# One attention order for two head pairs: read-outs in two groups, maxima through SyncE, more masks on TensorE

## The chip, the cores and the metric

One NeuronCore of a Trainium2 chip runs the whole program. The metric is the device time of one execution in microseconds; the median of three runs of the kernel before is 803.15 us (803.11 to 803.63).

## What is computed

A transformer block on 2048 rows of width 512, in four segments of 512 rows: attention with a compressive memory (32 heads of width 16), then a feed-forward part of width 1792. Cut to the part that the change touches:

```python
for s in range(N):                                   # 4 segments of L = 512 rows
    logits = einsum("bhqd,bhkd->bhqk", qs, ks) * scale + mask      # causal
    p = softmax(logits, axis=-1)
    a_dot = einsum("bhqk,bhkd->bhqd", p, vs)
    o = g * a_mem + (1.0 - g) * a_dot                # a_mem: read from the memory M, z
    M, z = M + phi(ks)^T vs, z + sum(phi(ks))
x = x + ga * (concat(o) @ wo)
h = layernorm(x) * (1 + cb) + sb
x = x + gb * (gelu(h @ w1 + b1) @ w2 + b2)
```

## The kernel before

The program has three stages: projections of q, k, v and the memory (0 to about 195 us), attention (about 180 to 485 us), and the feed-forward part. The change is in the attention stage. All engines run their instructions in the order in which the program writes them; nothing reorders them, so an instruction that waits holds everything behind it on its engine or its DMA queue.

**Units of work.** `P` numbers 64 head pairs (16 in each segment). `Q = P // 2` is two head pairs, so four heads; `U = Q // 2` is eight heads, a quarter of the width of one segment. q and k of one `Q` come from DRAM as bf16 stacks of 96 rows (`qst`, `kst`, 384 KB each, `load_stacks`); four buffers of each are used in turn.

**S, the scores for the maxima.** `s_part(P, n)` multiplies q rows by k columns into a PSUM bank of the ring `att` (six banks, taken in turn by S and T alike). Parts 0 and 1 are 128 query rows by 512 and by 384 keys, one bank for each head; part 2 is 256 keys and part 3 is 128 keys, both heads in one bank. VectorE takes the row maxima: either `masked_max` (one instruction for each head, which adds the mask itself, followed by a short read of the accumulator), or TensorE first adds the mask with a matmul of the identity by `maskb` and one `s_max` reduces both heads. `PRM["m"] = [0, 1, 0, 1]` chooses: the 128-key part goes by TensorE's mask, the 256-key part by `masked_max`. S of pair `P + 4` is written beside T of pair `P`.

**The maxima's way.** When all maxima of a `Q` are there, `m_rows` (GpSimd) splits them into three bf16 terms, `m_put` turns them by a matmul into the PSUM tile `mm`, ScalarE copies them to `ms`, and a DMA of 12 KB writes `ms` into rows 96 to 98 of `qst`. That DMA is issued by ScalarE (`act.dma_start`). The first T of that `Q` contracts over 99 rows and so waits for it.

**T, the transposed scores.** `st_part(P, n)`: parts 0 and 1 are the two heads with 128 keys by 512 queries, 2 and 3 by 384 queries, part 4 both heads by 256, part 5 both by 128. ScalarE takes the exponential into `pt`, GpSimd sets the upper triangle to zero.

**The read-out.** `pv_part(Q, j, ...)` multiplies `pt` of key block `j` by V, four heads side by side in 32 columns each, 8 matmuls for each `j`, added up in one PSUM tile `pv`; `pv_out` copies it to `ts` (ScalarE) and stores it to DRAM (`TD`). Then come `pv_in` (loads `dn`, `opk`, `amB`), `den`, `rb_in` (`rbB`), `mix`, `o_hi`, `o_lo`, on VectorE, GpSimd, ScalarE and SyncE's queue.

**The output product.** `wo_part(s, b, g)` is 3 matmuls; four of them (g = 0 to 3) make row block `b` of segment `s` in the tile `mm`; `wo_out` adds x on VectorE, or by ScalarE and GpSimd (`PRM["wout"]`), and stores to `X2D`. For segments 0 to 2 they lie within attention. `ln2_load`, `ln2_stats`, `ln2_apply`, `ln2_turn` prepare the feed-forward part of segments 0 and 1.

**What sets the order.** `PRM["order"]` has one row for even and one for odd `P` (per segment). A token `S0` to `S3`, `T0` to `T5` writes that part; `M3` writes the mask of a pending S part; `c0` to `c9` write whatever `todo` holds for that place of that `P`. Places are numbered 10 for each `P`, 20 for each `Q`; "place 25 + 20 Q" is `c5` of pair `2Q + 2`. I call the 20 places of one `Q` a slot. A step placed at `20 Q + d` lies in slot `Q + d // 20`.

Of the kernel before, what the change touches and what calls it, by code (L numbers as in the profile page):

```python
# [25 lines left out]
PRM = {'order': ['S0 c0 c1 T0 T1 S1 c2 T2 c3 c4 c5 T3 S3 c6 M3 S2 c7 c8 c9 T4 T5',  # L26
# [9 lines left out]
 'turn': 2,  # L36
# [4 lines left out]
 'pvout': [35, 35, 35, 35],  # L41
 'mrows': [-19, -20, -20, -20],
 'mput': [-9, -12, -12, -12],
 'stacks': -64,
# [6 lines left out]
 'wo': [[2, 10, 10, 10], [6, 10, 11, 11], [2, 10, 10, 11]],  # L51
 'woout': [10, 11, 11],
 'wox': [-23, -23, -23],
 'mixu': 13,
 'olou': 13,
 'ht': [463, 481, 501, 521],
 'ht1': 644,
 'ln': [[312, 339, 374, 408], [531, 566, 603, 624]],
# [29 lines left out]
 'm': [0, 1, 0, 1],  # L88
# [18 lines left out]
def block_kernel(ctx: ExitStack, tc: tile.TileContext, x, wq, wk, wv, wo, betaq, betam,  # L107
# [481 lines left out]
    with ExitStack() as pb:  # L589
# [34 lines left out]
        def s_part(P, part):  # L624
# [12 lines left out]
            else:  # L637
# [14 lines left out]
        pend = []  # L652

        def s_mask():
            if pend:
                pair, dst = pend.pop()
                n = pair.shape[2]
                pe.matmul(pair[:, :, n - 128:n], identb, maskb[:, 384:].unsqueeze(1).to_broadcast([128, 2, 128]),  # L658
                          start=False, stop=True)
                s_max(dst, pair)  # L660
# [16 lines left out]
        def m_put(Q):  # L677
            ns = nss.pop(Q)
            pe.matmul(mm[:, :128], top(ns.rearrange("q c n -> q (c n)")), identb, start=True, stop=True)
            ms = sb.tile([48, 128], BF16, tag="ms", bufs=2, name=f"ms{Q}")  # L680
            copy(PRM["mse"], ms, mm[:48, :128])
            act.dma_start(qst[Q % NK][96:99], ms)
# [115 lines left out]
        def o_hi(U):  # L798
            oh = so.tile([128, 512], F32R, tag="oh", bufs=5, name=f"oh{U}")
# [3 lines left out]
        def o_lo(U):  # L803
            ol = so.tile([128, 512], F32R, tag="ol", bufs=5, name=f"ol{U}")
# [125 lines left out]
        for Q in range(32):  # L930
            z = Q // 8
            pv = PRM["pv"][z]
            assert all(pv[0][0] <= x[0] <= pv[3][0] for x in pv) and PRM["pvout"][z] >= pv[3][0]
            ap(20 * Q + PRM["mrows"][z], m_rows, Q)
            ap(20 * Q + PRM["mput"][z], own, "mm", ("m", Q), m_put, (Q,), True)
            for i, (d, j, lo, hi) in enumerate(pv):
                ap(20 * Q + d, own, "pv", Q, pv_part, (Q, j, lo, hi, i == 0, i == 3), False)
            ap(20 * Q + PRM["pvout"][z], own, "pv", Q, pv_out, (Q,), True)
        for U in range(16):
            z = U // 4  # L940
            ap(40 * U + 20 + PRM["pvout"][z] + PRM["dnl"], pv_in, U)
            if U == 15:
                ap(40 * U + 20 + PRM["pvout"][z] + PRM["dnl"], am_in, U)
            ap(40 * U + PRM["den"][z], den, U)
            ap(40 * U + PRM["den"][z] + PRM["rbl"] + (5 if U == 14 else 0), rb_in, U)
            assert 20 + PRM["pvout"][z] + PRM["dnl"] <= PRM["den"][z] and PRM["den"][z] + PRM["rbl"] <= PRM["mix"][z]
# [3 lines left out]
            ap(40 * U + PRM["ohi"][z], o_hi, U)  # L950
            ap(40 * U + PRM["olo"][z], o_lo, U)
            assert PRM["den"][z] <= PRM["mix"][z] <= PRM["ohi"][z] <= PRM["olo"][z]
        for s in range(NSEG - 1):
            for b in range(4):
                e = 160 * s + 230 + 20 * b
                ap(e + PRM["wox"][s], wo_x, s, b)
                if s < 3:
                    assert PRM["wo"][s] == sorted(PRM["wo"][s]) and PRM["woout"][s] >= PRM["wo"][s][3]
                    for i, d in enumerate(PRM["wo"][s]):
                        ap(e + d, own, "mm", (s, b), wo_part, (s, b, i), False)  # L960
                    ap(e + PRM["woout"][s], own, "mm", (s, b), wo_out, (s, b), True)
        assert all(y[0] <= x <= y[3] < 0 for y in PRM["vl"] for x in y)
        assert PRM["wl"] == sorted(PRM["wl"]) and PRM["gate"] > PRM["wl"][1] + 60
        for i, (ln, ld) in enumerate(zip(PRM["ln"], PRM["lnd"])):
            assert ln[0] > 160 * i + 290 + PRM["woout"][i] and ln[1] > ln[0]
# [24 lines left out]
        for d in range(KB):  # L990
            ap(PRM["ht"][d], own, "mm", ("h", d), ln2_turn, (0, d), True)
            ap(PRM["ht1"], lambda d: ln2_turn(1, d, bank("att")), d)
        for P in range(-LEAD, NP + 2):
            if P in PRM["w1at"]:
                load_w1(PRM["w1at"].index(P))
            for tok in PRM["order"][2 * min(P // 16, 3) + P % 2 if P >= 0 else 8 + P % 2].split():
                n = int(tok[1])
# [409 lines left out]
```

## Time and profile before

| | |
|---|---|
| median of 3 runs | 803.15 us |
| the profiled execution's own time | 803.54 us |
| its span, first to last instruction | 801.8 us |
| mean granted TensorE clock | 0.994 |
| busy: TensorE / VectorE / ScalarE / GpSimd | 782.6 / 557.9 / 464.9 / 336.2 us |
| DMA | 156.10 MB, 195 GB/s over the span |

1.7 us of the execution's time lie outside the span. Durations of matmuls overlap: the end of each is modelled and holds the way through the array, so what a matmul costs is read as the distance from its start to the next start.

### The profile page before, as it was taken

What the parts mean: (1) busy time and instruction counts of PE and PEld (TensorE: products, weight loads), DVE (VectorE), ACT (ScalarE), POOL (GpSimd) and SP (SyncE); (2) the same over time, 40 slices, a digit from 0 to 9 for tenths busy, and PEclk for the clock granted to TensorE, in tenths of its full rate; (3) what the DMA queues carried; (4) which work ended last, traced back from release to release, by engine and by line L of the source; (5) the groups of instructions that cost most, each with busy time, mean ns of one, the idle gap of its engine ahead of it and who ended that gap; (6) DMA issues with size and microseconds to landing.
All of it is one profiled execution on the core that took longest, in us unless ns stands there. A gap on an engine that the chain in (4) does not pass through costs nothing.

```text
span 801.8 us, 14163 instructions
## 1 busy us (share of the span) xinstructions
PE 782.6 (98%) x4585; PEld 532.0 (66%) x4585; DVE 557.9 (70%) x1411; ACT 464.9 (58%) x912; POOL 336.2 (42%) x556
## 2 busy tenths in 40 slices
PE   9999999999999999999999998989999999999998
PEld 4877777876444455445544555768888888888887
DVE  6686697459888877697778779866659866533423
ACT  3465545465778766675678574757745336653221
POOL 1347366451478555567866586133000404400000
PEclk9999999999999999999999999999999999999999
DMA  9597857495565676768557854584575644445443
GB/s 339 183 318 233 284 181 233 149 331 170 147 195 164 187 209 174 219 179 216 155 175 203 233 160 147 173 283 155 192 255 176 195 136 158 158 145 171 156 134 117
DMA packets 108818, 156.10 MB, mean 195 GB/s; under 512 B 16324, under 2 KB 55620, under 8 KB 108744
## 3 DMA queue, kind: packets, MB, share of 16 engines
q1 hardware_dynamic: 106248, 153.23, 60.7%
q10 hardware_dynamic: 2496, 1.97, 0.8%
q8 instruction: 36, 0.59, 0.3%
q14 instruction: 38, 0.31, 0.1%
HBM read 93.95 MB, written 60.83 MB: 193 GB/s over the span
## 4 chain that ended last, share of the span: by engine, by line
PE 76%; ACT 7%; DMA 6%; DVE 6%; issue 3%; POOL 1%; SPq 1%; ACTq 0%; DVEq 0%; POOLq 0%
PE pv L740 8%; PE bx L1059 7%; PE att L700 7%; PE att L611 6%; PE q L318 5%; PE bx L1324 5%; PE by L1324 4%; PE bv L1324 4%; PE k L318 4%; PE mm L817 4%; PE bv L1059 4%; PE v L469 3%; DMA qst<-ms 2%; PE spare L1324 2%; ACT pt L715 2%
## 5 line engine op out<-in xcount | busy, mean ns | idle before, releaser
L618 DVE CUSTOM_DVE_ANT_0 dump<-att,maskb 128x512 bf16<-128x512 f32 (+2 forms) x384 | 192.3, 553 | 27.0 <-PE att L611 24.8
L715 ACT ACTIVATE pt<-att 128x512 f32<-128x512 f32 (+1 forms) x256 | 126.1, 558 | 47.0 <-PE att L700 44.3
L703 POOL TENSOR_SCALAR_AFFINE_SELECT pt<-pt 128x256 f32<-128x256 f32 x256 | 101.9, 416 | 82.5 <-ACT pt L715 51.6
L700 PE MATMUL att<-qst,kst 99*128 99x512 bf16 (+3 forms) x512 | 106.8, 301 | 5.6 <-DMA qst<-ms 3.5
L611 PE MATMUL att<-kst,qst 96*128 96x512 bf16 (+2 forms) x384 | 94.3, 327 | 1.7 <-DMA qst<-QD 1.4
L740 PE MATMUL pv<-pt,V 128*32 128x512 f32 (+2 forms) x992 | 88.2, 446 | 0.0
L854 POOL TENSOR_TENSOR wb<-wa 128x256 f32<-128x256 f32 x24 | 21.0, 876 | 154.9 <-DMA wa<-in_w 148.9
L700 PEld LDWEIGHTS <-kst 99*128 99x128 bf16 x512 | 42.9, 97 | 57.6 <-issue 38.7
L726 ACT ACTIVATE pt<-att 128x512 f32<-128x512 f32 (+1 forms) x128 | 57.2, 514 | 21.6 <-PE att L611 19.6
L611 PEld LDWEIGHTS <-qst 96*128 96x128 bf16 x384 | 33.2, 98 | 40.7 <-issue 23.8
L141 DVE TENSOR_TENSOR gl<-s,gh 128x512 fp32r<-128x512 f32 x34 | 24.5, 721 | 42.0 <-ACT gh L138 42.0
L138 ACT ACTIVATE gh<-s 128x512 fp32r<-128x512 f32 x34 | 21.3, 628 | 47.2 <-PE spare L1324 17.1
L740 PEld LDWEIGHTS pv<-pt,V 128*32 128x32 f32 x992 | 22.1, 108 | 36.4 <-issue 26.1
L622 DVE TENSOR_REDUCE nm<-att 128x2 f32<-128x256 f32 x64 | 27.2, 425 | 22.1 <-PE att L658 17.7
L1064 ACT ACTIVATE s<-s,b1t 128x512 f32<-128x512 f32 x42 | 30.2, 720 | 18.6 <-DVE s L1068 18.6
L1068 DVE TENSOR_TENSOR s<-bv,s 128x512 f32<-128x512 f32 x28 | 19.2, 688 | 25.5 <-PE bv L1059 20.2
L618 DVE DVE_READ_ACCUMULATOR2_ANT nm<- 128x1 f32 x384 | 31.9, 83 | 0.0
L514 POOL TENSOR_TENSOR q<-qr,q 128x512 bf16<-128x512 f32 x16 | 18.7, 1167 | 26.7 <-ACT q L513 26.3
L505 POOL TENSOR_SCALAR qp<-qp 128x512 f32<-128x512 f32 x12 | 19.1, 1594 | 24.0 <-ACT qp L500 24.0
L141 DVE TENSOR_TENSOR w1ml<-s,w1mh 128x512 fp32r<-128x512 f32 x18 | 13.0, 721 | 21.5 <-ACT w1mh L138 21.5
L318 PE MATMUL q<-Ahh,wqh 128*128 128x512 f32 x64 | 25.9, 405 | 0.4 <-DVE Ahh L140 0.4
L138 ACT ACTIVATE w1mh<-s 128x512 fp32r<-128x512 f32 x18 | 11.3, 628 | 25.6 <-PE spare L1324 13.1
(364 smaller groups left out, 2112.7 us busy)
## 6 DMA issues: line engine op xcount, KB each, us to landing
GD<-s SPq DMA_DIRECT2D x56, 256.0 KB
s<-GD SPq DMA_DIRECT2D x52, 256.0 KB
kst<-KD SPq DMA_DIRECT2D x32, 384.0 KB
qst<-QD SPq DMA_DIRECT2D x32, 384.0 KB
TD<-ts SPq DMA_DIRECT2D x32, 256.0 KB
xt<-X2D SPq DMA_DIRECT2D x28, 256.0 KB
wa<-in_w SPq DMA_DIRECT2D x28, 256.0 KB
QD<-q SPq DMA_DIRECT2D x16, 384.0 KB
```

What stands on the lines that cost most here:

```text
L138: act.activation(hi, src, AF.Copy)
L141: lo_eng.tensor_tensor(out=lo, in0=src, in1=hi.bitcast(F32), op=ALU.subtract)
L318: pe.matmul(ps, a[:, k, 128 * g:128 * g + 128], b[k], start=(k == 0 and i == 0), stop=(k == KB - 1 and i == 2))
L611: pe.matmul(ps, q_of(P, h, i), k_of(P, h, 128 * (i + 1)), start=True, stop=True)
L618: v.tensor_tensor_reduce(out=dump[n_dump[0] % 2][:, :n], in0=src, in1=maskb[:, 512 - n:], scale=-1.0, scalar=-4 * NEG, op0=ALU.add, op1=AL ...
L700: pe.matmul(ps, k[:99, e, 128 * j:128 * j + 128], q[:99, e, 128 * j:512], start=True, stop=True)
L703: pool.affine_select(out=t, in_=t, pattern=pattern, compare_op=ALU.is_ge, fill=0.0, base=0, channel_multiplier=-1)
L715: act.activation(pt[:, h, :], ps[:, :n], AF.Exp, scale=0.25)
L726: act.activation(pt, pv_, AF.Exp, scale=0.25)
L740: pe.matmul(ps[32 * c:32 * c + 32, lo:hi], V[4 * s + j][:, VW * hd:VW * hd + 32], pt[:, c % 2, lo - o:hi - o], start=start, stop=stop)
L1059: pe.matmul(ps, a[:, i, k, :], b[k], start=start and k == 0 and c == 0, stop=k == 1 and c == 2, skip_group_check=not start)
L1324: pe.matmul(ps, a[:, c], w[:, lo:hi], start=(f == 0 and i == 0), stop=(last and i == 2))
```

## The change

One order string for a whole `Q` takes the place of the ten rows, with 20 places. Within it the T parts of the second kind (`T2`, `T3`, by 384 queries) of the first pair come first in the slot, and the 512-query parts of the second pair last. Beside that:

- read-outs (`pv`): key block 0 at place 31 + 20 Q (`c11` of the next slot), blocks 1, 2, 3 at 36, 37, 38 (`c16` to `c18`, adjacent); for the last `Q` the row of the old segment 3 stays;
- masks: `m = [0, 0, 0, 1]`, and the last entry only from `Q = 14` on, so that the 256-key part goes by TensorE's mask and one `s_max` for all first pairs and for second pairs of `Q < 14`; the mask matmul now follows its S matmuls at once (`pend` and `M3` are gone);
- `m_rows` at 20 Q - 21, `m_put` at 20 Q - 13 (before: -19 or -20, and -9 or -12); `m_put` uses the tile `pv` in place of `mm`, and the DMA is issued by SyncE (`sp.dma_start`);
- stacks are loaded at 20 Q - 60 in place of 20 Q - 64;
- output product: parts at `c2` and `c5` of each of eight slots for segments 0 and 1 (before: four parts in each of four slots); for segment 2 four parts in each of four slots, at `c2`, `c5`, `c8`, `c14`; `wo_out` follows at the next place;
- `ln2` steps of segment 0 move later, and `ln2_turn(0)` takes banks of `att` in place of `mm`; `oh` and `ol` get six buffers in place of five; `o_hi` and `o_lo` of U = 6 and 10 come 16 places later.

```diff
-PRM = {'order': ['S0 c0 c1 T0 T1 S1 c2 T2 c3 c4 c5 T3 S3 c6 M3 S2 c7 c8 c9 T4 T5',
-           'T0 S0 c0 c1 c2 S1 c3 T2 T3 T1 S2 c4 c5 T4 S3 M3 T5 c6 c7 c8 c9',
...
+ORDER = ('S1 c0 T2 T3 T2 c1 S2 c2 S3 T3 S3 c3 c4 c5 T5 S0 c6 c7 T0 c8 c9 '
+         'T1 T4 S2 c10 c11 T5 S1 c12 T4 S0 c13 T0 c14 T1 c15 c16 c17 c18 c19')
...
- 'pv': [[[25, 0, 0, 512], [32, 1, 128, 512], [31, 2, 256, 512], [34, 3, 384, 512]],
...
- 'mrows': [-19, -20, -20, -20],
- 'mput': [-9, -12, -12, -12],
- 'stacks': -64,
+ 'pv': [[31, 0, 0, 512], [36, 1, 128, 512], [37, 2, 256, 512], [38, 3, 384, 512]],
+ 'pvlast': [[25, 0, 0, 512], [30, 1, 128, 512], [31, 3, 384, 512], [35, 2, 256, 512]],
+ 'mrows': -21,
+ 'mput': -13,
+ 'stacks': -60,
...
- 'wo': [[2, 10, 10, 10], [6, 10, 11, 11], [2, 10, 10, 11]],
+ 'wo': [[20 * i + o for i in range(8) for o in (2, 5)]] * 2 + [[20 * i + o for i in range(4) for o in (2, 5, 8, 14)]],
...
- 'm': [0, 1, 0, 1],
+ 'm': [0, 0, 0, 1],
+ 'mq': 14,
...
-                if PRM["m"][2 * p + i]:
+                if PRM["m"][2 * p + i] and Q >= PRM["mq"]:
...
-                pend.append((pair, nm[:, p, :, i:i + 1]))
...
                 pe.matmul(pair[:, :, n - 128:n], identb, maskb[:, 384:].unsqueeze(1).to_broadcast([128, 2, 128]),
                           start=False, stop=True)
-                s_max(dst, pair)
+                s_max(nm[:, p, :, i:i + 1], pair)
...
         def m_put(Q):
             ns = nss.pop(Q)
-            pe.matmul(mm[:, :128], top(ns.rearrange("q c n -> q (c n)")), identb, start=True, stop=True)
+            ps = bank("pv")
+            pe.matmul(ps[:, :128], top(ns.rearrange("q c n -> q (c n)")), identb, start=True, stop=True)
             ms = sb.tile([48, 128], BF16, tag="ms", bufs=2, name=f"ms{Q}")
-            copy(PRM["mse"], ms, mm[:48, :128])
-            act.dma_start(qst[Q % NK][96:99], ms)
+            copy(PRM["mse"], ms, ps[:48, :128])
+            sp.dma_start(qst[Q % NK][96:99], ms)
...
+        for Q in range(-LEAD // 2, NP // 2 + 1):
...
+            seen = {}
+            for tok in ORDER.split():
+                n = int(tok[1:])
+                if tok[0] == "c":
+                    for f, a in todo.pop((2 * Q + n // 10, n % 10), ()):
                         f(*a)
+                    continue
+                P = 2 * Q + seen.get(tok, 0)
+                seen[tok] = 1
+                if tok[0] == "S" and P + LEAD < NP:
+                    s_part(P + LEAD, n)
+                elif tok[0] == "T" and 0 <= P < NP:
+                    st_part(P, n)
```

On TensorE, this is the order before in the first segment, where a read-out of 256 columns, the turning of the maxima and a read-out of 384 columns follow each other between S parts.

```order
L611 MATMUL att_2067<-kst_1833,qst_1832 128x512
L740 MATMUL pv_2068<-pt_2_2327,V_197 32x256 x2
L740 MATMUL pv_2068<-pt_2_2381,V_197 32x256 x2
L679 LDWEIGHTS nm_2057
L679 MATMUL mm<-identb,nm_2057 128x128
L740 MATMUL pv_2068<-pt_1_2309,V_196 32x384 x2
L740 MATMUL pv_2068<-pt_1_2360,V_196 32x384 x2
L611 LDWEIGHTS qst_1832
L611 MATMUL att_2062<-kst_1833,qst_1832 128x384
```

And this is the end of a slot on TensorE now (`pt_1`, `pt_2`, `pt_3` are the key blocks 1 to 3; L683 is T and L601 is S).

```order
L683 MATMUL att_2064<-qst_2075,kst_2076 128x512
L723 MATMUL pv_2068<-pt_1_2299,V_196 32x384 x2
L723 MATMUL pv_2068<-pt_1_2305,V_196 32x384 x2
L723 MATMUL pv_2068<-pt_2_2342,V_197 32x256 x2
L723 MATMUL pv_2068<-pt_2_2364,V_197 32x256 x2
L723 MATMUL pv_2068<-pt_3_2323,V_198 32x128 x2
L723 MATMUL pv_2068<-pt_3_2355,V_198 32x128 x2
L601 LDWEIGHTS qst_1837
L601 MATMUL att_2065<-kst_1838,qst_1837 128x384
```

Three of the four key blocks now stand together, and the turning of the maxima stands between S and T matmuls.

On SyncE's queue, this is before a piece of a slot in which a row block of the output product is stored (`X2D`); the maxima are not on this queue.

```order
L751 DMA TD_3761<-ts_3885 128x512
L180 DMA kst_2076<-KD_1_98 96x2048
L180 DMA qst_2075<-QD_1_82 96x2048
L836 DMA X2D_121<-xb_3_3702 128x512
L756 DMA dn_3945<-TD_3761 128x1x32
L758 DMA opk_3947<-TD_3761 128x1x512
```

This is such a piece now, in an odd slot of the segment.

```order
L734 DMA TD_4232<-ts_4354 128x512
L170 DMA kst_2076<-KD_3_100 96x2048
L170 DMA qst_2075<-QD_3_84 96x2048
L819 DMA X2D_121<-xb_3_4107 128x512
L665 DMA qst_1832<-ms_4409 3x16x128
L739 DMA dn_4415<-TD_4232 128x1x32
L741 DMA opk_4417<-TD_4232 128x1x512
```

The transfer of the maxima (L665) has come into this queue, behind the two stack loads and the store of the output block.

On VectorE, this is what stands ahead of that store now: the last reduction of S parts 2 and 3, the two masked maxima of S part 0, and the addition for the output block (`xb`).

```order
L612 TENSOR_REDUCE nm_2055<-att_2067 128x2
L608 ISA dump_2070,nm_2055<-att_2063,maskb 128x512
L608 ISA nm_2055 128x1
L608 ISA dump_2069,nm_2055<-att_2064,maskb 128x512
L608 ISA nm_2055 128x1
L818 TENSOR_TENSOR xb_3_4107<-mm,xb_3_4107 128x512
```

Before, the same addition stands behind two maxima of S part 0 as well.

```order
L622 TENSOR_REDUCE nm_2054<-att_2063 128x2
L618 ISA dump_2070,nm_2055<-att_2065,maskb 128x512
L618 ISA nm_2055 128x1
L618 ISA dump_2069,nm_2055<-att_2066,maskb 128x512
L618 ISA nm_2055 128x1
L835 TENSOR_TENSOR xb_3_3702<-mm,xb_3_3702 128x512
```

What has moved is who stands behind it: before the store alone, now the store and the maxima of a `Q`.

More of the change, by code (lines that the diff above doesn't have):

```diff
@@ L949, in block_kernel @@
             assert PRM["mmix"] <= PRM["mix"][z]
[L950 to L951 removed]
+            late_by = PRM["olate"] if U in (6, 10) else 0
+            ap(40 * U + PRM["ohi"][z] + late_by, o_hi, U)
+            ap(40 * U + PRM["olo"][z] + late_by, o_lo, U)
             assert PRM["den"][z] <= PRM["mix"][z] <= PRM["ohi"][z] <= PRM["olo"][z]
@@ L954, in block_kernel @@
             for b in range(4):
[L955 to L961, printed above, removed]
+                w = [160 * s + 240 + i for i in PRM["wo"][s][4 * b:4 * b + 4]]
+                ap(w[0] + PRM["wox"], wo_x, s, b)
+                assert w == sorted(w)
+                for i, d in enumerate(w):
+                    ap(d, own, "mm", (s, b), wo_part, (s, b, i), False)
+                ap(w[3] + 1, own, "mm", (s, b), wo_out, (s, b), True)
         assert all(y[0] <= x <= y[3] < 0 for y in PRM["vl"] for x in y)
@@ L990, in block_kernel @@
         for d in range(KB):
[L991 removed]
+            ap(PRM["ht"][d], lambda d: ln2_turn(0, d, bank("att")), d)
             ap(PRM["ht1"], lambda d: ln2_turn(1, d, bank("att")), d)
[L993 to L997, printed above, removed]
[L998 to L1008 removed]
+        for Q in range(-LEAD // 2, NP // 2 + 1):
+            for k, P in enumerate(PRM["w1at"]):
+                if P // 2 == Q:
+                    load_w1(k)
+            seen = {}
[3 more added lines that the diff above has]
+                    for f, a in todo.pop((2 * Q + n // 10, n % 10), ()):
+                        f(*a)
+                    continue
[5 more added lines that the diff above has]
+                    st_part(P, n)
     left = [(f.__name__, a[0] if a else None, lambda f=f, a=a: f(*a)) for P, part in sorted(todo)
```

48 lines of the change are left out of this document (16 added, 32 removed), and 11 rows, old and new, of the table PRM.

## The prediction

> **What bounds the kernel now.** I read the page first, then who waits on TensorE, then the attention stage row by row. The page's first line:
>
> ```profile
> PE 782.6 (98%) x4585; PEld 532.0 (66%) x4585; DVE 557.9 (70%) x1411; ACT 464.9 (58%) x912; POOL 336.2 (42%) x556
> ```
>
> TensorE sets the time, but 98% says little, because modelled ends hide short stalls. So I go by distances from start to start. These rows of the timeline are from one plain slot (no output product), from a first read-out at 259.87 to the next one at 267.73, and the row below them is the same stretch by windows (its length, then busy times):
>
> ```profile
> 259.87 1.06 PE L740 MATMUL pv<-pt,V 128*32 128x512 f32 x8
> ...
> 261.15 0.27 PE L658 MATMUL att<-maskb,identb 128*128 128x256 bf16 x1
> 261.27 0.38 PE L611 MATMUL att<-kst,qst 96*128 96x256 bf16 x2
> 261.49 0.22 PE L679 MATMUL mm<-identb,nm 128*128 128x128 bf16 x1
> 261.55 0.71 PE L700 MATMUL att<-qst,kst 99*128 99x256 bf16 x5
> 262.09 0.60 PE L611 MATMUL att<-kst,qst 96*128 96x512 bf16 x2
> 262.62 1.28 PE L740 MATMUL pv<-pt,V 128*32 128x256 f32 x16
> 263.83 0.50 PE L611 MATMUL att<-kst,qst 96*128 96x384 bf16 x2
> ...
> 265.95 0.59 PE L611 MATMUL att<-kst,qst 96*128 96x512 bf16 x2
> 266.39 0.38 PE L700 MATMUL att<-qst,kst 99*128 99x512 bf16 x1
> 266.93 0.38 PE L700 MATMUL att<-qst,kst 99*128 99x512 bf16 x1 [0.16 <-ACT pt L726]
> ```
>
> ```profile
> 259.87:267.73 7.86, 7.70 (x69) 3.54 (x68) 6.92 (x28) 6.11 (x15) 3.92 (x12) 1.00 0.55 170
> ```
>
> Two 512-column S matmuls take 0.44 us from 265.95 to 266.39, so 0.22 each; the mask matmul, half as wide, takes 0.12 (261.15 to 261.27), and by its width 0.11, the turning of the maxima 0.06. The only stall is before 266.93: 0.54 after the start before it, so 0.32 lost, because the six-bank ring has come round to a bank that ScalarE has not emptied. The slot lasts 7.86 us, of which 7.54 is TensorE's own work. The other losses are single waits:
>
> ```profile
> PE att L700 <- DMA qst<-ms: 3.5, 4, 2.0
> ...
> PE att L700 <- ACT pt L726: 1.7, 9, 0.3
> PE att L611 <- DMA qst<-QD: 1.4, 1, 1.4
> ```
>
> The first is T waiting for the maxima (4 times), the second the ring wait (9 times), the third S waiting for a stack. Each shows 0.16 too little, the part of a 0.38 us matmul that lies beyond its 0.22. After the longest wait for the maxima the granted clock (last column but two) is down:
>
> ```profile
> 333.80:337.20 3.40, 3.34 (x14) 0.74 (x15) 1.31 (x5) 1.47 (x3) 0.77 (x2) 0.61 0.99 311
> 337.20:340.00 2.80, 2.80 (x28) 1.61 (x28) 1.95 (x8) 1.29 (x4) 0.41 (x1) 0.86 0.12 32
> ```
>
> That costs another 3.4 x 0.39 + 2.8 x 0.14 = 1.7 us. So the old stalls come to 9 x 0.32 = 2.9 (ring), 3.5 + 4 x 0.16 = 4.1 (maxima), 1.6 (stack) and 1.7 (clock): 10.3 us. They, and the work itself, are what the change can take from.
>
> **The change part by part: the read-outs.** In the first segment (Q = 0 to 7) the read-outs stand in four groups a slot; the middle two:
>
> ```profile
> 205.62 0.64 PE L740 MATMUL pv<-pt,V 128*32 128x256 f32 x8
> 206.19 0.23 PE L679 MATMUL mm<-identb,nm 128*128 128x128 bf16 x1
> 206.36 0.85 PE L740 MATMUL pv<-pt,V 128*32 128x384 f32 x8
> 207.14 0.50 PE L611 MATMUL att<-kst,qst 96*128 96x384 bf16 x2
> ```
>
> Apart they take 0.57 + 0.78 = 1.35 us to the next other matmul; together (262.62 to 263.83) 1.21. So a group's end costs 0.14. Its beginning costs 0.09: the two S matmuls ahead of it take 0.53 (262.09 to 262.62) where they take 0.44 elsewhere. One group fewer saves 0.23. From four to two in 8 slots and from three to two in 23 slots (the last Q is left as it was) is 39 groups: **-9.0 us**, all on the path, since TensorE has no cover.
>
> **The masks.** 46 head pairs (32 first ones, 14 second ones) get a mask matmul: 46 x 0.11 = **+5.1 us** on TensorE, and nothing hides it. VectorE gives up two masked maxima for one reduction of twice the size:
>
> ```profile
> L618 DVE CUSTOM_DVE_ANT_0 dump<-att,maskb 128x512 bf16<-128x512 f32 x128 | 83.1, 687 | 6.2 <-PE att L611 4.6 <-POOL pt L703 1.5
> L618 DVE CUSTOM_DVE_ANT_0 dump<-att,maskb 128x384 bf16<-128x384 f32 x128 | 66.1, 554 | 20.8 <-PE att L611 20.2
> L618 DVE CUSTOM_DVE_ANT_0 dump<-att,maskb 128x256 bf16<-128x256 f32 x128 | 48.8, 419 | 0.0
> ...
> L835 DVE TENSOR_TENSOR xb<-mm,xb 128x512 f32<-128x512 f32 x9 | 6.2, 691 | 7.1 <-PE mm L817 6.1 <-DMA TD<-ts 1.0
> ```
>
> A reduction over 512 is not in the trace; between one masked maximum of 512 (0.69) and two of 256 (0.84) it saves 0 to 0.15. VectorE is not what ends the slot, so I count nothing.
>
> **The output product.** 192 matmuls before and now, in 24 more groups, since parts stand alone. In the chain of waits three matmuls alone take 0.75 and nine together 2.06:
>
> ```profile
> 367.04 0.75 PE mm L817 x3
> 368.25 2.06 PE mm L817 x9
> ```
>
> 0.75 - 0.69 = 0.06 a group; from 0 to 0.06, 24 x 0.05 = **+1.2 us**.
>
> **The ring waits.** Walked through with a matmul's cost in proportion to its columns, the new order meets one bank that may not be empty: the second pair's second T of 384 queries needs the bank of the first pair's S of 384, whose two maxima end 0.33 + 0.03 + 2 x 0.55 = 1.46 after the slot's first matmul (a 384 matmul lasts 0.50 - 0.17 = 0.33 by the row at 263.83; 0.03 is the hand-over from 261.49 + 0.22 to the copy at 261.74, quoted below), while TensorE is there at 1.38. That is 0.1, in the 12 slots that have no output product at `c2` ahead of it: +1.2. The old ring wait (T of 512 queries behind the exponential of 256) goes, since the exponentials now come in an even stream and the copy of the read-out falls at the slot's end, where ScalarE has nothing else: **-2.9 + 1.2**.
>
> **The maxima.** The transfer and what it now stands behind, with the issue times on both queues before:
>
> ```profile
> 261.74 0.27 ACT L132 ACTIVATE ms<-mm 48x128 bf16<-48x128 f32 x1
> 262.04 0.73 ACTq L682 DMA_DIRECT2D qst<-ms  x1
> ```
>
> ```profile
> 304.27 0.34 SPq L836 DMA_DIRECT2D X2D<-xb  x1
> ```
>
> ```profile
> 222.96 3.40 DMA qst<-ms
> ...
> 327.38 6.44 DMA qst<-ms
> ...
> 436.48 7.80 DMA qst<-QD
> ```
>
> ScalarE loses an issue of 0.73 us per Q; it is not the bound, so this is in the ring's term. From the turning (261.49) to the issue (262.04) is 0.55. From the issue to the first T that needs it was 4.35 in this slot (to 266.39). Now the turning is at `c7`. Ahead of it in the slot stand S of 384 (0.33), three T of 384 (0.50), S of 256 and its mask (0.33), two S of 128 with masks (0.44), T of 384 and of 128 (0.28) and S of 512 (0.44), together 2.3 us. The slot's work is 7.54 - 0.23 + 0.11 = 7.42 where one mask is added; from the turning to the first T of the next slot it is 7.42 - 2.3 + 0.33 = 5.45, so 4.9 after an undisturbed issue. That is more than before, and where a transfer took 3.40 nothing waits. But in the eight odd slots that end an output block in segments 0 and 1, SyncE first waits with the store of that block: VectorE gets to the addition after two maxima of 512, 0.38 + 0.03 + 0.69 + 0.69 + 0.69 = 2.48 after the start of that S part, 2.04 after the turning; with 0.34 for the store's issue the maxima leave at 2.4, and 3.05 us are left. Against 3.40 (light traffic) this is a wait of 0.35, against 6.44 (four loads of 256 KB beside it) 3.4. I take the light row, because the loads of `ln2` stand in one of those slots at most: 8 x 0.35 = +2.8; ends 0 and 27. Behind the waiting store stand also `dn`, `opk`, `amB`, which are used more than ten places later. Old waits for the maxima and the clock loss go: **-5.8 + 2.8**.
>
> The Trainium skill bears on this in "DMA: Bandwidth & Descriptors", section "Queues, rings and completion order": each DMA engine takes turns between the rows of SyncE and ScalarE packet by packet, and within a row takes descriptors in ring order. By that the maxima now start behind every stack byte still queued, where before they had turns of their own. No row here shows a small transfer on SyncE's queue behind a large one; by that rule the 8 waits would lie above 0.35.
>
> **The stacks.** Loaded 20 places before their first use, not 24: the worst took 7.80 from issue to use. A plain slot, less the read-out's copy and three issues ahead at 0.34, leaves some 6 us (an estimate from these rows), so a wait as before can come; **-1.6 + 1.6**.
>
> **Sum** against the profiled 803.5: -9.0 + 5.1 + 1.2 - 2.9 + 1.2 - 5.8 + 2.8 - 1.6 + 1.6 = -7.4, so 796.1; the median of the runs shown is 0.4 lower: **795.7 us**. The feed-forward part and the last pairs are counted at nothing.
>
> **The rivals.** *No new waits at all*: without 1.2, 2.8 and 1.6 the sum is -13.0, 790.1. For it: VectorE and ScalarE have slack in a plain slot, and 4.9 us exceed most transfers. Against: the old kernel had such waits with less in SyncE's queue.
>
> *New waits take the place of the old ones, one for one*: only the work changes, -9.0 + 5.1 + 1.2 = -2.7, 800.4. For it: the ring has six banks as before and the same instructions fill it.
>
> *The maxima in SyncE's queue, slower*: if each of the eight slots waits 2.1 us as at 333.8, and the clock falls each time, they cost 8 x (2.1 + 1.7) = 30.4 in place of 2.8, and the time is 823.3. It turns into a loss from (803.5 - 793.3) / 8 = 1.3 us a slot. For it: the row of 6.44, and GpSimd does every other addition of segment 1 behind its own work. Against: in the row of 6.44 the loads were issued in the same microsecond; they are elsewhere in seven of the eight.
>
> The Trainium skill, "TensorE: Matmul & The Clock Gate", "Part 1: The HAM clock gate", has the clock halved only after an idle window of about 3.4 us. The trace differs: a wait of 2.0 shown was enough. By the page's figure this rival would cost 8 x 2.1 = 16.8 and end at 810.
>
> **How the numbers follow.** Forecast 0.58 (793 to 800), no new waits 0.17, one for one 0.12, the slow rival 0.13. A measurement of this kernel can tell about 0.2% (1.6 us), so faster means below 801.5. Of the one-for-one case about half falls within 0.2%, of the slow rival a little: faster 0.82, same 0.06, slower 0.12. The range 788.5 to 803.5 holds the first three cases and the weak end of the fourth; below 790 it allows for a saving at the last pairs.
>
> **What would show it.** In the profile after: two groups of read-outs a slot (x8 and x24); plain slots of about 7.6 us from read-out to read-out; slots of 8.8 with output parts; 110 mask matmuls on TensorE; no rows of T waiting for ScalarE in most slots. In the odd slots from 13 to 27, T waits of 0.3 us for the maxima, and no half clock. I am wrong if T waits for `ms` by more than a microsecond in most of those slots, if S waits for stacks in plain slots, or if the plain slots stay near 7.9 us because other bank waits have come.

## The result, and the profile after

| | before | after |
|---|---|---|
| median | 803.39 us (4 runs) | 812.49 us (4 runs, 808.45 to 814.69) |
| ratio | | 1.0103, 95% interval 1.0061 to 1.0146 |
| profiled execution, span | 803.54, 801.8 | 808.45, 806.7 |
| first read-out of the first to that of the last `Q` | 202.93 to 482.58 = 279.7 | 205.79 to 490.08 = 284.3 |

Slower by 1.0%, where 795.7 us was forecast. Three single executions well above the others of their kernel (814.5 us in adds_vector, 1093 and 4090 us in spread_early) are left out of the ratios below. The traced execution is the fastest of its four, so the account below explains 808.45 us; what made the other three up to 6 us longer is not known.

The loss lies in attention. The first read-out stands six places later than before, so the last row of the table, 4.6 us of the 4.9 us of span, does not compare like with like. From the first T (195.55 us before, 196.30 after) to the first output product of the last segment (484.87 and 492.37) it is 289.3 and 296.1 us, so attention lost 6.8 us. The part behind that took 2.6 us less (314.4 for 316.9), with the same matmuls. The first line of the page after reads:

```profile
PE 780.6 (97%) x4631; PEld 540.7 (67%) x4631; DVE 553.5 (69%) x1273; ACT 476.6 (59%) x912; POOL 334.9 (42%) x556
```

TensorE has 46 more matmuls and is busy for less; its idle time has grown. A plain stretch of the timeline, from the first read-out of one `Q` to that of the next, shows the new order at work:

```profile
274.37 1.06 PE L723 MATMUL pv<-pt,V 128*32 128x512 f32 x8
...
277.00 1.50 PE L723 MATMUL pv<-pt,V 128*32 128x384 f32 x24
...
279.70 0.27 PE L640 MATMUL att<-maskb,identb 128*128 128x256 bf16 x1
280.00 0.32 PE L683 MATMUL att<-qst,kst 99*128 99x384 bf16 x1
```

The same stretch, and one with output parts, in the windows (length, busy times, third from the end the granted clock):

```profile
274.37:282.07 7.70, 7.68 (x71) 3.91 (x70) 6.40 (x22) 6.88 (x17) 5.79 (x14) 1.00 0.72 213
308.60:317.57 8.97, 8.97 (x75) 4.64 (x74) 7.55 (x26) 7.00 (x16) 6.63 (x14) 1.00 0.68 199
```

Two groups of read-outs (x8 and x24), 7.70 us where it was 7.86, and 8.83 or 8.97 with output parts: what the forecast said of an ordinary slot has come. The only bank wait in the plain stretch is the one walked through there, 280.00 - 279.70 - 0.11 = 0.19. The loss is in a few long stretches. "Stretch Q" below runs from the first read-out of `Q` to that of `Q` + 1; it ends in slot Q + 2.

| stretch | 3 | 7 | 11 | 19 | 20 | 22 | 26 | 27 |
|---|---|---|---|---|---|---|---|---|
| before | 8.10 | 7.86 | 10.40 | 10.41 | 10.44 | 9.19 | 11.95 | 10.69 |
| after | 13.27 | 7.70 | 8.83 | 10.72 | 10.08 | 13.25 | 10.10 | 13.99 |

(Output parts are spread over other stretches than before, so single pairs differ by their work too; 3 and 7 have none in either.) Who waits on TensorE:

```profile
PE att L601 <- DMA qst<-QD: 7.0, 4, 2.6
PE att L683 <- DMA qst<-ms: 3.2, 3, 2.6
PE att L683 <- ACT pt L709: 2.0, 2, 1.1
...
PE pv L662 <- POOL nm L656: 1.3, 1, 1.3
```

Before, S waited once for a stack, 1.4 us; now four times, 7.0. The worst is in stretch 3. SyncE's queue there, before:

```profile
226.78 0.43 SPq L180 DMA_DIRECT2D qst<-QD  x1
228.70 0.35 SPq L902 DMA_DIRECT2D wor<-in_wo  x1
```

and after:

```profile
229.12 0.36 SPq L885 DMA_DIRECT2D wor<-in_wo  x1
...
230.48 0.50 SPq L170 DMA_DIRECT2D qst<-QD  x1
```

The stacks used to be issued at c16, ahead of the rows of `wo` (`wor`, c17); at c0 of the next slot they stand behind them. That load needs a buffer, which ScalarE and GpSimd give back late (SyncE's waits from 222 to 231 us):

```profile
SPq L885 <- ACT woh L891: 3.5, 1, 3.5
SPq L885 <- POOL pt L686: 2.8, 1, 2.8
```

The chain of waits shows the end of it, and the window behind it shows the clock at half for 6.83 us:

```profile
230.48 5.62 DMA qst<-QD
...
236.15 0.82 PE att L601 x2
```

```profile
235.63:242.46 6.83, 6.31 (x27) 3.60 (x27) 3.80 (x11) 3.42 (x9) 3.49 (x5) 0.50 0.64 188
```

In stretch 19 the four loads of x (`xt`, 256 KB each) stand ahead of the stacks in the same way, in stretch 27 the reads for the next `mix` and two loads of `xt`:

```profile
366.34 1.84 SPq L551 DMA_DIRECT2D xt<-X2D  x4
...
370.18 0.31 SPq L170 DMA_DIRECT2D qst<-QD  x1
```

The long wait for the maxima is in stretch 22. GpSimd normalises rows for the feed-forward part (L563), adds x to an output block (L816), and only then can SyncE store that block and send the maxima behind it:

```profile
401.72 2.07 POOL L563 TENSOR_SCALAR xt<-xt,cmv,crs 128x512 f32<-128x512 f32 x1
...
404.12 1.28 POOL L816 TENSOR_TENSOR xb<-xo,xb 128x512 f32<-128x512 f32 x1
```

```profile
405.42 0.34 SPq L819 DMA_DIRECT2D X2D<-xb  x1
405.82 0.80 SPq L665 DMA_DIRECT2D qst<-ms  x1
```

```profile
405.82 2.25 DMA qst<-ms
```

The transfer itself (the row of the chain) took only 2.25 us. In stretches 10 and 20 an exponential comes late because ScalarE, in order, first copies `oh` and waits for GpSimd's mix; here stretch 20:

```profile
384.39 0.63 ACT L122 ACTIVATE oh<-opk 128x512 fp32r<-128x512 f32 x1 [1.30 <-POOL opk L774]
384.93 0.85 ACT L709 ACTIVATE pt<-att 128x256 f32<-128x256 f32 x2
```

### The profile page after: what moved, and what is told of

Its sections match the earlier page's. It is cut to its first block, busy times and chain, and to the rows that moved or that the text cites. A ratio compares the mean times of both kernels' runs of the same rounds, so it can differ in the third digit from the quotient of the medians.

```text
span 806.7 us, 14047 instructions
## 1 busy us (share of the span) xinstructions
PE 780.6 (97%) x4631; PEld 540.7 (67%) x4631; DVE 553.5 (69%) x1273; ACT 476.6 (59%) x912; POOL 334.9 (42%) x556
## 3 DMA queue, kind: packets, MB, share of 16 engines
q10 hardware_dynamic: 864, 1.57, 0.5%
## 4 chain that ended last, share of the span: by engine, by line
PE 77%; DMA 8%; DVE 4%; POOL 3%; ACT 3%; issue 3%; SPq 1%; DVEq 0%; ACTq 0%; POOLq 0%
PE bx L1043 7%; PE att L683 7%; PE pv L723 7%; PE bx L1308 5%; PE q L308 5%; PE att L601 5%; PE by L1308 5%; PE bv L1308 5%; PE k L308 4%; PE bv L1043 4%; PE mm L800 4%; PE v L459 3%; PE spare L1308 2%; PE mm L1308 2%; PE by L1043 2%
## 5 line engine op out<-in xcount | busy, mean ns | idle before, releaser
L608 DVE CUSTOM_DVE_ANT_0 dump<-att,maskb 128x512 bf16<-128x512 f32 (+1 forms) x292 | 159.2, 594 | 51.8 <-PE att L601 22.2
L698 ACT ACTIVATE pt<-att 128x384 f32<-128x384 f32 (+1 forms) x256 | 125.3, 543 | 25.8 <-PE att L683 23.2
L683 PE MATMUL att<-qst,kst 99*128 99x256 bf16 (+3 forms) x512 | 109.8, 305 | 5.8 <-DMA qst<-ms 3.2
L683 PEld LDWEIGHTS <-kst 99*128 99x128 bf16 x512 | 44.3, 99 | 71.6 <-issue 41.3
L601 PE MATMUL att<-kst,qst 96*128 96x512 bf16 (+1 forms) x292 | 77.6, 348 | 7.6 <-DMA qst<-QD 7.0
L723 PE MATMUL pv<-pt,V 128*32 128x512 f32 (+1 forms) x992 | 79.6, 439 | 0.0
L709 ACT ACTIVATE pt<-att 128x256 f32<-128x256 f32 (+1 forms) x128 | 61.6, 491 | 20.5 <-PE att L683 19.8
L612 DVE TENSOR_REDUCE nm<-att 128x2 f32<-128x256 f32 (+1 forms) x110 | 56.3, 533 | 12.5 <-PE att L640 9.9
L601 PEld LDWEIGHTS <-qst 96*128 96x128 bf16 x292 | 23.8, 99 | 17.2 <-DMA qst<-QD 8.6
L640 PE MATMUL att<-maskb,identb 128*128 128x256 bf16 x110 | 30.4, 283 | 0.0
L122 ACT ACTIVATE ts<-pv 128x512 f32<-128x512 f32 x31 | 18.5, 597 | 16.9 <-PE pv L723 14.5
L638 PE MATMUL att<-kst,qst 96*128 96x128 bf16 (+1 forms) x110 | 27.7, 252 | 0.0
```

The lines of the kernel that those rows point to most:

```text
L601: pe.matmul(ps, q_of(P, h, i), k_of(P, h, 128 * (i + 1)), start=True, stop=True)
L608: v.tensor_tensor_reduce(out=dump[n_dump[0] % 2][:, :n], in0=src, in1=maskb[:, 512 - n:], scale=-1.0, scalar=-4 * NEG, op0=ALU.add, op1=AL ...
L612: v.tensor_reduce(out=dst, in_=src, axis=AX.X, op=ALU.max, negate=True)
L683: pe.matmul(ps, k[:99, e, 128 * j:128 * j + 128], q[:99, e, 128 * j:512], start=True, stop=True)
L698: act.activation(pt[:, h, :], ps[:, :n], AF.Exp, scale=0.25)
L709: act.activation(pt, pv_, AF.Exp, scale=0.25)
```

## The experiments

Ratios are to the kernel before on the same chip, with 95% intervals. The runs stand on four chips, on which the median of the kernel before lies between 803.0 and 803.8 us; a difference of medians across chips is good to about 1 us.

| run | median us | ratio |
|---|---|---|
| after_again | 811.08 | 1.0102 (1.0067 to 1.0138) |
| stacks_early | 825.85 | 1.0286 (1.0252 to 1.0319) |
| maxima_act | 810.64 | 1.0104 (1.0066 to 1.0141) |
| both_back | 824.42 | 1.0259 (1.0226 to 1.0291) |
| loads_apart | 808.08 | 1.0053 (1.0030 to 1.0077) |
| adds_vector | 805.72 | 1.0019 (0.9997 to 1.0040) |
| three_moved | 802.38 | 0.9987 (0.9966 to 1.0007) |
| masks_back | 807.76 | 1.0068 (1.0046 to 1.0090) |
| queue_spread | 794.44 | 0.9873 (0.9844 to 0.9901) |
| spread_masks | 791.52 | 0.9845 (0.9815 to 0.9876) |
| readouts_four | 821.64 | 1.0212 (1.0174 to 1.0250) |
| old_order_sp | 816.02 | 1.0157 (1.0117 to 1.0197) |
| spread_act | 800.20 | 0.9959 (0.9941 to 0.9978) |
| spread_early | 806.63 | 1.0024 (0.9999 to 1.0049) |

**after_again**: no edit.

> The changed kernel once more, unaltered, so that the other kernels of this batch can be compared with it on the same chip. Both theories expect 808 to 815 us, and again a few large waits instead of slower work: three waits of S for a stack of q (7.0 us in the first profile, near 236, 377 and 459 us), one of T for the maxima of about 2.8 (near 408), and the granted clock down for some microseconds behind the longest of them; plain slots of 7.7 us.

811.08 us; stretches 3, 19, 22 and 27 are again the long ones (11.56, 11.01, 11.51, 13.92). So the waits belong to the program's places, not to one execution.

**stacks_early.**

```diff
- 'stacks': -60,
+ 'stacks': -64,
```

> Stacks loaded at 20 Q - 64 as before, four places earlier, at c16 of a slot: ahead of the weights of the output product (c17), of the loads of x for the feed-forward part (c17) and of the store TD, where at 20 Q - 60 they stand behind these on SyncE's queue. Theory A (the stacks' new place behind other loads on that queue is what costs): the three waits of S for a stack (7.0 us) and the half clock behind them (some 5 to 6 us) go, the time falls by 8 to 13 us, to 797 to 803 us. Theory B (the maxima on SyncE's queue hold that queue up, and the stacks with it): four places change nothing, since the transfers of the maxima stand where they stood; the waits for stacks stay at 5 to 8 us in all and the time within 4 us of the changed kernel's.

Neither theory foresaw this. In stretch 3, where `wor` had stood ahead, 9.33 us are left of 13.27, so there theory A held; but the time rose by 15 us. SyncE's queue in a plain slot shows why:

```profile
268.98 0.41 SPq L170 DMA_DIRECT2D kst<-KD  x1
269.44 0.41 SPq L170 DMA_DIRECT2D qst<-QD  x1
269.95 0.37 SPq L734 DMA_DIRECT2D TD<-ts  x1
...
275.97 0.62 SPq L739 DMA_DIRECT2D dn<-TD  x1
```

Now the store `TD` stands behind 768 KB of stacks, and `dn`, which reads what it stored, holds SyncE until 275.97, 6.0 us after the store was issued. Such waits of L739 between 205 and 490 us, here and in the changed kernel:

```profile
SPq L739 <- DMA TD<-ts: 31.2, 12, 5.6
```

```profile
SPq L739 <- DMA TD<-ts: 4.8, 3, 2.4
```

So the next `RD`, `rbB`, stacks and maxima all go out later, and T waits for the maxima in slots where nothing waited:

```profile
PE att L683 <- DMA qst<-ms: 9.3, 9, 3.6
PE att L601 <- DMA qst<-QD: 7.4, 6, 3.7
```

**maxima_act.**

```diff
- sp.dma_start(qst[Q % NK][96:99], ms)
+ act.dma_start(qst[Q % NK][96:99], ms)
```

> The transfer of the maxima issued by ScalarE as before, all else as in the changed kernel. Theory A (the stacks' place): the waits for stacks stay at 5 to 8 us; the one large wait of T for the maxima (2.8 us near 408, where the transfer stood behind a late store of an output block) goes with its half clock, 2 to 5 us, and ScalarE's issues of 0.7 us cost up to 0.3 a slot in ring waits: 805 to 813 us. Theory B (the maxima on SyncE's queue hold up what is behind them): both kinds of wait go, 797 to 803 us.

810.64, no change, within theory A's range. The wait for the maxima in stretch 22 is gone (10.58 us for 13.25). Of the four waits for stacks three are left, 4.8 us in all for 7.0, so most of it does not come from the maxima on SyncE's queue; a part may. Most undisturbed stretches became longer: 7.81 to 7.91 for 7.70, 9.10 for 8.83, 9.51 for 8.97. The last of these, 0.5 us, is more than the 0.3 a slot that I had allowed for ScalarE's issue of 0.7 us.

**both_back**: both edits.

> Stacks at 20 Q - 64 and the maxima issued by ScalarE, both as before, all else as in the changed kernel. Theory A: as with the stacks alone, and the wait for the maxima near 408 goes too: 794 to 800 us. Theory B: as with the maxima alone, 797 to 803 us. If neither holds, and the new order itself makes the stalls, it stays above 806 us.

824.42: neither theory's number, and above the 806 us of the third case, the new order itself; queue_spread below shows that this is not the cause. With the stacks early the loss is the same, within the intervals, whichever queue sends the maxima.

**loads_apart**: the one-time loads move (those of x stood at 397, four at once, and at 531, 535, 551, 555), the stacks stay at -60.

```diff
- 'wl': [17, 66, 80, 81],
+ 'wl': [25, 66, 80, 81],
- 'lnl': [0, 4, 20, 24],
+ 'lnl': [[312, 352, 354, 392], [531, 535, 551, 572]],
- ap(ln[0] + PRM["lnl"][b] * i, ln2_load, i, b)
+ ap(PRM["lnl"][i][b], ln2_load, i, b)
```

> Maxima and stacks as in the changed kernel; only loads that come once move on SyncE's queue: the rows of wo eight places later (c5 in place of c17), the four loads of x of segment 0 one at a time in the slots before in place of four together at place 397, and the last of segment 1 from 555 to 572. With the stacks four places earlier the wait of S at the first of these places had gone, but the stacks then stood ahead of the store TD, and everything else became slower. Theory A2: the three big waits of S for a stack (2.5, 2.2 and 2.1 us) come from the one-time loads that stand just ahead of the stack loads; they fall below 0.8 us each, the half clock behind two of them goes too, and the time falls by 8 to 12 us, to 799 to 803 us. Rival: the transfers are simply too many in those stretches, or SyncE's waits for the read-out's copy hold the stacks; then two of the three waits stay above 1.5 us and the time stays above 807 us. The wait for the maxima near 407 us (2.7 us) stays in either case.

808.08, a gain of 3 us against after_again and not 8. At two of the three places theory A2 held: stretch 3 takes 8.07 us and 19 takes 8.83. In stretch 27 (11.98, where it was 13.92) a wait of 1.6 us is left; only one of the two loads of `xt` ahead of those stacks had been moved, so this run does not show what holds them there. T now waits 2 us for the maxima at 478 us (stretch 29: 11.26 for 7.68). They were issued just behind two loads of weights for the feed-forward part (`wa`) and took 5.20 us; the load moved to 572 had gone out 15 us earlier:

```profile
470.88 1.11 SPq L825 DMA_DIRECT2D wa<-in_w  x2
```

```profile
472.95 5.20 DMA qst<-ms
```

The wait in stretch 22 was 3.7 us long this time:

```profile
PE att L683 <- DMA qst<-ms: 6.5, 4, 3.7
```

**adds_vector.**

```diff
- 'wout': ['vvvv', 'vava', 'vava'],
+ 'wout': ['vvvv', 'vvvv', 'vvvv'],
```

> The additions of x to the output blocks all on VectorE, none on GpSimd (every other one of segments 1 and 2 before). If T's wait near 407 us is late because the store of the block, with GpSimd's addition behind its own mixing, stands ahead of the maxima on SyncE's queue, the wait (2.7 us and 1.9 us of half clock) goes, and with it the wait for GpSimd's splitting of the maxima near 472 (1.4 us): 5 us less, 804 to 808 us. If it is the transfer itself that takes long there, the wait stays and the time is within 2 us of the changed kernel's.

805.72: 5 us, as expected. Stretch 22 takes 9.46 us for 13.25. So the late store ahead of the maxima was the cause there, not the transfer.

**three_moved**: both of these, and

```diff
- 'ohi': [110, 110, 110, 111],
- 'olo': [110, 110, 110, 116],
+ 'ohi': [115, 115, 115, 111],
+ 'olo': [115, 115, 115, 116],
```

> The moved loads, the additions on VectorE, and the splitting of o into high and low parts five places later (ScalarE waited 1.3 us for GpSimd's mix ahead of an exponential twice, which gave ring waits of 1.0 and 1.4 us). If the loss against the forecast is only these few collisions, the sum is 811 - 10 - 5 - 2.5: 792 to 797 us, below the kernel before. If each wait that goes lets another come in its place, 800 us or more.

802.38: better by 9 us, but not the 792 to 797 of my sum; it is the other case, in which new waits come. The ring waits behind `oh` are gone (stretch 20 takes 8.83 us). But S waits 2.0 us for a stack in stretch 10, T waits 3.3 us for the maxima at 475 us, again just behind the two loads of `wa`, and at 405 us TensorE waits 2.4 us for GpSimd, which makes `ol` (five places later now) just ahead of splitting the maxima:

```profile
403.51 1.26 POOL L789 TENSOR_TENSOR ol<-opk,oh 128x512 fp32r<-128x512 f32 x1
404.73 0.51 POOL L656 TENSOR_TENSOR nm<-nm 128x16 f32<-128x16 f32 x2
```

**masks_back**: masks as before.

```diff
- 'm': [0, 0, 0, 1],
- 'mq': 14,
+ 'm': [0, 1, 0, 1],
+ 'mq': 0,
```

> Masks as before: 64 mask matmuls in place of 110, VectorE adds the mask for the 256-key part. By the forecast's term 46 x 0.11 us of TensorE come back and VectorE has room: 5 us less, 804 to 808 us, and plain slots of 7.48 us in place of 7.70. Rival: two masked maxima hold the bank longer than one reduction, and the ring makes TensorE wait for VectorE instead: plain slots of 7.7 us or more, the same time or slower.

807.76: 3.3 us less. Plain stretches of 7.62, not 7.48: two mask matmuls (0.22) go, and the wait that was 0.19 grows to 0.26. It is the same wait as before, for the two masked maxima of S of 384 keys: T starts 1.57 us after that S part in both kernels (278.43 to 280.00 in the changed one, 276.49 to 278.06 here), only TensorE is there earlier. So this is not the longer hold that the rival named. A last 0.07, in smaller gaps, I have not explained.

**queue_spread**: the same cures, with the places chosen anew.

```diff
- 'wl': [17, 66, 80, 81],
+ 'wl': [25, 66, 80, 81],
- 'wox': -25,
+ 'wox': -34,
- 'ohi': [110, 110, 110, 111],
- 'olo': [110, 110, 110, 116],
+ 'ohi': [115, 115, 115, 111],
+ 'olo': [121, 121, 121, 116],
- 'wout': ['vvvv', 'vava', 'vava'],
+ 'wout': ['vvvv', 'vvvv', 'vvvv'],
- 'lnl': [0, 4, 20, 24],
+ 'lnl': [[288, 328, 368, 408], [528, 532, 551, 568]],
- ap(ln[0] + PRM["lnl"][b] * i, ln2_load, i, b)
+ ap(PRM["lnl"][i][b], ln2_load, i, b)
- ap(ln[3] + ld[1] * b, ln2_apply, i, b, (pool, v)[i])
+ ap(ln[3] + ld[1] * b, ln2_apply, i, b, v)
```

> The rows of wo at c5, the loads of x for the feed-forward part one at a time at c8 of even slots (behind the maxima, ahead of nothing that is waited for soon), x for the output blocks at c8 in place of c17, all additions and the normalising of segment 0 on VectorE, the high part of o five places later and the low part behind the splitting of the maxima. If the loss is a handful of collisions on SyncE's and GpSimd's queues in the new order, no wait over 1 us is left between 205 and 470 us and the time is 790 to 796 us, below the kernel before. If spreading only shifts the waits (the queue has no slack left with the maxima on it), it stays at 800 us or more.

794.44 us: what was forecast for the change as it stood. Stretches 3, 10, 19, 20 and 22 take 8.07, 8.83, 8.82, 8.84 and 8.83. Between the first read-out and the last no wait is longer than 1.0 us as shown; of those on the maxima and stacks this is left:

```profile
PE att L601 <- DMA qst<-QD: 3.1, 5, 1.0
...
PE att L683 <- DMA qst<-ms: 0.5, 1, 0.5
```

**spread_masks**: queue_spread with the masks of before.

> The same with masks as before (64 mask matmuls in place of 110). By the slots without big waits, 7.62 against 7.70 and 8.73 against 8.83, the masks on TensorE cost 0.1 us a slot: 2 to 3 us below the run before it. If VectorE is late at other places then, equal or slower.

791.52, 2.9 us below queue_spread, and the fastest of all: 1.5% below the kernel before.

**readouts_four.**

```diff
- 'pv': [[31, 0, 0, 512], [36, 1, 128, 512], [37, 2, 256, 512], [38, 3, 384, 512]],
+ 'pv': [[31, 0, 0, 512], [32, 1, 128, 512], [33, 2, 256, 512], [38, 3, 384, 512]],
```

> The changed kernel with the read-outs in four groups a slot (c11, c12, c13, c18) in place of two, everything else unchanged. The forecast's price of a group, 0.23 us, gives plain slots of 7.70 + 0.46 = 8.16 and 31 x 0.46 = 14 us more: 822 to 828 us. If the price is not in the groups but in what stood beside them, plain slots stay at 7.7 to 7.9 and the time below 818 us.

821.64, 10.6 us more than after_again: just below the range, since some long stretches were shorter this time (3 takes 11.49 for 13.27, 27 takes 12.35 for 13.99). In stretch 29, which has neither S parts nor bank waits, with four groups and with two in the changed kernel:

```profile
488.25:496.41 8.16, 8.16 (x62) 3.76 (x61) 3.98 (x7) 6.16 (x14) 5.97 (x11) 1.00 0.47 156
```

```profile
476.48:484.17 7.69, 7.69 (x62) 4.05 (x61) 4.25 (x7) 6.06 (x14) 6.72 (x11) 1.00 0.54 164
```

0.47 for two groups, 0.23 each, as forecast. With output parts it is 0.24 each (9.32 for 8.83). In plain stretches two groups cost 0.78 (8.48 for 7.70), of which 0.27 are a new bank wait of an S part (0.38 from the start before it, 0.11 in the changed kernel), so 0.25 each.

**old_order_sp**: one part alone, in the kernel before.

```diff
- act.dma_start(qst[Q % NK][96:99], ms)
+ sp.dma_start(qst[Q % NK][96:99], ms)
```

> One part alone: the kernel before with the maxima issued by SyncE in place of ScalarE. In the new order this took 0.1 to 0.5 us off each slot that has no big wait (7.70 against 7.80 to 7.91, 8.83 against 9.10), since ScalarE is held 0.7 us by each issue. If that holds in the old order too, its plain slots fall from 7.86 to 7.6 us and the time by 3 to 7 us, to 796 to 800. If SyncE's queue cannot take it, T waits for the maxima behind the stores of the output blocks and the time is 806 us or more.

816.02, slower by 1.6%. Plain stretches did not change (7.86), and T waits ten times for the maxima:

```profile
PE att L700 <- DMA qst<-ms: 11.8, 10, 2.8
```

Their place on the queue, near 392 us:

```profile
390.88 0.46 SPq L765 DMA_DIRECT2D amB<-AMD  x1
391.38 0.43 SPq L826 DMA_DIRECT2D xb<-in_x  x1
391.85 0.79 SPq L682 DMA_DIRECT2D qst<-ms  x1
```

```profile
391.85 5.69 DMA qst<-ms
```

Here they stand behind the loads of `opk`, `amB` and `xb`, 256 KB each, and take 5.69 us; in the new order they are issued at c7, ahead of the loads at c9. So in the old order, with its places as they were, the move is a loss.

**spread_act**: queue_spread with the maxima sent by ScalarE.

> The kernel with the spread queue (794 us), and the maxima issued by ScalarE again. If the maxima on SyncE's queue are a loss of their own in the new order (theory B), this is faster, 788 to 792 us. If they are a gain there, as the undisturbed slots say (7.70 with SyncE, 7.80 to 7.91 with ScalarE; 8.83 and 9.10; 8.97 and 9.50), it is slower by some 30 x 0.2 = 6 us: 798 to 802 us.

800.20: 5.8 us slower than with SyncE. Undisturbed stretches take 7.85 and some 9.1 in place of 7.70 and 8.83. Theory B is out: with the queue spread, the maxima on SyncE are a gain.

**spread_early**: queue_spread with the stacks at -64.

> The kernel with the spread queue, and the stacks loaded at 20 Q - 64 again. If the place of the stacks is a loss of its own (theory A as first stated), the last waits for stacks (3.1 us) go: 790 to 792 us. If the 768 KB of a stack pair ahead of the store TD delay TD, dn behind it, and the maxima behind these, as the first run with -64 suggests (TD took 6.7 us there at the median, 3.8 at -60), it is slower by 8 us or more: 802 us or more.

806.63: 12 us slower, and SyncE again waits for `TD` (in queue_spread 3 times, 4.3 us in all):

```profile
SPq L739 <- DMA TD<-ts: 30.0, 14, 4.4
```

So of the two places tried c0, behind `TD`, is the better one for the stacks in a plain slot. What cost was the work that comes once and stood around that place.

## Why the prediction was wrong

**The read-outs** (-9.0): right. 0.23 us a group was measured again.

**The masks** (+5.1): right in TensorE's work, 0.11 us for each mask matmul. Taking them back gained only 3.3 and 2.9 us: in a plain slot 0.07 of the 0.22 us returns as a wait for VectorE, and 0.07 in gaps not explained. Since the changed kernel does carry the 46 matmuls, the term stays in the sum below.

**The output product** (+1.2) and the length of the slots (7.6 and 8.8): the slots took 7.70 and 8.83 to 8.97, as forecast. The +1.2 was not tested apart.

**The ring waits** (-2.9 + 1.2): the new wait is where it was said, 0.19 in place of 0.1 us, in eight slots. Seven smaller bank waits that I had not walked through (four of 0.2 to 0.3 us, three of 0.13) came beside it; all fifteen make 2.8 us. Not seen: ScalarE held by `oh` (L122) ahead of an exponential, 1.2 us each in stretches 10 and 20 (10.02 and 10.08 against 8.83 and 8.84 in queue_spread). The step `ohi` keeps its number, but c10 now stands ahead of other parts than c0 of the next pair did; I walked TensorE's banks and not ScalarE's own list.

**The maxima** (-5.8 + 2.8): the mechanism was right, a store waiting ahead of them on SyncE's queue. The price was not. In six of the eight slots the maxima left 2.3 us after the turning, once 2.6 and once 3.6 (2.4 in my sum), T began 2.3 to 4.3 us after that, and it did not wait; in four of the six this is less than the 3.40 us that I took for the transfer. One of the eight had the small wait (0.4 with the 0.16 added), and so had one slot without a store. One waited 2.6 us with half clock behind it (4.4 us against queue_spread). I had named GpSimd's additions in segment 1 as what could make it worse, and had not put the one beside L563. The slow rival came true in this one slot; in the old order ten such waits came, 11.8 us in all.

**The stacks** (-1.6 + 1.6): this is the step that failed. I wrote that "a plain slot, less the read-out's copy and three issues ahead at 0.34, leaves some 6 us" and "a wait as before can come". For plain slots that was right. But the step had moved past c17, where loads that come once are issued, and I never listed what else stands at the places in between. I put the term at one wait as before, 1.6 us. The runs showed four waits instead, 7.0 us, with half clock behind two of them: in stretches 3, 19, 26 and 27 the changed kernel took 5.2 + 1.9 + 0.6 + 2.9 = 10.6 us more than queue_spread, clock included, which is 9.0 above my term. For 3 and 19 loads_apart shows the cause, for 26 and 27 it is argued from the queue alone.

**The sum again**: 796.1 + 9.0 (stacks) + 2.4 (maxima: 4.4 + 2 x 0.4, less 2.8) + 2.4 (`oh`) + 1.2 (stretch 28, GpSimd's splitting of the maxima) + 1.6 (bank waits, 2.8 less 1.2) + 0.8 (up to the first T) - 2.6 (the feed-forward part, which I had counted at nothing) = 810.9 us, where the profiled run took 808.45. The rest, 2.5 us, stays open. That the cause is collisions of this kind and not the new order as such, is shown by queue_spread: the same order, read-outs, masks and queues, and 794.44 us. That its median lies 1.3 us from the forecast is in part luck: its feed-forward part, too, is 2.8 us shorter than before.

The rival that all stalls return one for one (800.4) had the right shape and too low a price, because three of the new stalls (stretches 3, 22 and 27) drew a half clock. My first theory on the result, that the stacks' place itself was wrong, fell too.

## What to carry to other kernels

When a step moves along an in-order queue, list every instruction that it passes over the whole program, the ones that come once too, with what each of them waits for: the plain slot is not where it fails. A DMA issue that waits for another DMA (`dn` on `TD`) makes the landing time of a store a matter of the whole queue, so large loads go behind such a store and not ahead of it. When a change loses although its steady state gained, compare the long stretches one by one, and move what collides there, before taking the change back.

## What the runs showed of the hardware

A queue of its own did not make a small transfer quick. In spread_act the 12 KB of maxima, sent by ScalarE 0.6 us after SyncE had issued the second of two stack loads, took

```profile
222.29 6.24 DMA qst<-ms
```

and on SyncE's queue in stacks_early, 1.8 us after the second of two stack loads,

```profile
338.85 6.27 DMA qst<-ms
```

while 405.82 above, 0.4 us behind one store of 256 KB and 7.5 us behind the last stack load, took 2.25. The Trainium skill, "DMA: Bandwidth & Descriptors", "Queues, rings and completion order", has each DMA engine take turns between the two engines' rows; by that I had expected ScalarE's row to be the safer one. The two rows above show no such advantage.

How much of the clock a wait costs depends on where it falls. In the changed kernel the granted clock fell to half at 235.63, 409.71 and 460.91 us, for 6.83, 3.41 and 3.41 us; the distances between these times are 51 and 15 times 3.413. In the 3.41 us before each fall TensorE was idle for 2.1, 1.8 and 2.0 us (by the modelled ends). Here is the third fall, in stretch 27:

```profile
457.50:460.91 3.41, 1.46 (x10) 1.03 (x11) 1.16 (x6) 1.29 (x4) 0.28 (x2) 1.00 0.20 48
460.91:464.32 3.41, 3.41 (x15) 2.03 (x14) 1.52 (x5) 0.98 (x3) 0.92 (x3) 0.50 0.85 263
```

The wait of 1.8 us in stretch 19 fell across a boundary of these 3.41 us steps. Only 1.7 us of idle time lay in the second of the two, and the clock stayed:

```profile
375.57:378.98 3.41, 1.75 (x11) 1.18 (x11) 1.28 (x5) 1.56 (x4) 0.25 (x2) 1.00 0.23 57
378.98:382.39 3.41, 3.41 (x27) 1.95 (x29) 3.21 (x10) 2.23 (x6) 0.65 (x1) 1.00 0.81 259
```

I counted the same in the 15 traces that have such a fall between 150 and 780 us. All falls of a trace lie whole steps apart. Of the steps at full clock, all 33 with more than 1.85 us of idle TensorE were followed by half clock, none of the 2693 with less than 1.66 us was, and of the 14 in between 6 were. So in this program a TensorE idle for about half of one step loses the clock for at least the next one. The wait that ended at 236 us made stretch 3 longer by 5.2 us against queue_spread, twice its own 2.6 us.
